# One core, a two-layer convolution and feed-forward kernel: its first filter block loaded in two transfers, and a new hand-written issue order

## The chip, the cores and the metric

The kernel runs on one core of one Trainium2 chip. The metric is device time in microseconds (us) of one execution; three runs of the kernel before took 343.04, 343.35 and 342.95 us, and the median, 343.04 us, is the number that counts. Engine names are those of the profile: PE is TensorE's matmul side and PEld its weight loads, DVE is VectorE, ACT is ScalarE, POOL is GpSimd and SP is SyncE, which here issues nearly all the DMAs.

## The reference

Activations `x` are 2048 rows of 512. Two identical layers are applied, each with a long convolution (A) and a feed-forward net (B):

```
def _A_ref(q, k, v, shift_k, ssm_k, ssm_D):
    k_shift = sum over t of k_pad[:, t:t + S, :] * shift_k[:, ks - 1 - t]      # 4 taps
    kv = k_shift * v
    y = irfft(rfft(pad(kv)) * rfft(pad(ssm_k)))[:S]                            # causal, length S
    return q * (y + kv * ssm_D)
def _B_ref(x, w_gate, w_up, w_down):
    return (silu(x @ w_gate) * (x @ w_up)) @ w_down

x = A_q
x = x + _A_ref(_layernorm(x), A_k, A_v, A_shift_k, A_ssm_k, A_ssm_D)
x = x + _B_ref(_layernorm(x), B_w_gate, B_w_up, B_w_down)
(the same two lines once more)
```

The two convolutions differ only in their multiplier, the normalised `x`: the filtered `y` is the same in both layers.

## The kernel before

The sequence is cut into four blocks of 512 rows, `c` = 0 to 3. A block of 512 rows lies in a tile as 128 partitions times 4 interleaved rows `r` = 0 to 3. For each block the kernel makes spectra of the filter `h` (tiles `hn`, transposed to `hs`, spectrum `H` or `G`) and of `kv` (tiles `kn`, `kTb`, `vt`, spectrum `X`), multiplies them on DVE (`t`, `Z`), goes back with a second table of sines (`inv`), and gets `Yk`. A layer norm, the product with `Yk` and a second layer norm give `z`; its transpose `zT` is what the feed-forward matmuls read. The feed-forward net runs over 16 units (layer, block, half); its gate and up matmuls write PSUM tiles `pf`, which ACT evacuates to `sg` and `ht`, DVE multiplies the two, and the down matmuls accumulate in `pd`. The spectra of the later blocks are worked out beside the feed-forward units of the earlier ones; only block 0 stands ahead of everything.

**Block 0, the part that the change touches.** SP issues the loads in this order: `h` of block 0 (`load_h`, L346 to L354, one transfer of 512 KB: 128 partitions, four pieces of 512 columns, one piece for each of the four groups `dt` of 128 channels), `k` (`load_k`, L364), `v` (`load_v`, L394), the activations (L398), `h` and `v` of block 1, and `w_gate`. ACT issues the small taps `tapR` and the vector `drow`. PE first turns the taps (L1173), then transposes `h` (L489): 16 transposes of 128x128, for rows `r` in the order 0, 2, 3, 1 four at a time, one for each `dt`. A row's four transposes fill one PSUM tile, which DVE or ACT copies to `hs` (rows 0 and 1 on DVE, rows 2 and 3 on ACT). Then come 16 transposes of `k` (L378), four for each `dt`, each four copied to `kTb` (L384 on ACT, L386 on DVE).

Two kinds of matmuls follow. The eight "products of `h`" (function `half`, L323 with `hs` and `fwd`) are two matmuls of 512 columns each; four of them read rows 0 and 2, four rows 1 and 3; their results are evacuated to `ev` and combined by four butterflies on DVE into `G` (L457 and L459). The 64 matmuls of the short convolution (function `shift_mul`, L323 with `dg` and `kTb`, 128 columns each, 16 for each row) are multiplied into `vt` on DVE (L536, one for each row). From `vt` come 16 pairs of matmuls for the spectrum `X` (function `direct`, L470), and from `X` and `G` the chain of block 0 described above, up to `zT` (L940 on ACT, L938 on DVE) and the first gate or up matmul.

**What sets the order.** The kernel is written as a list of 1556 operations, in the order of the `add` calls. Each has an engine, a cost and, for a DMA, a latency (`LH0` 3.6 for the first `h`, `LK0` 4.3 for the first `k`, 6.6 for the first `v`). A table `ORDER` gives every operation its place, and the operations are issued in that order, so each engine's instruction stream is written out by hand; costs and latencies do not reach the chip, with one exception. `issue` puts dummy matmuls on PE (tile `wm`, L1307, operands of ones) where the planned start of an operation lies more than 0.5 us behind the end of the one before it on PE:

```
if start < warm_until and start - t > 0.5:
    ...
                n = int((start - t - (0.35 if 0.0 < t < 8.0 else 0.3)) / 0.106)
                if n > 0:
                    warm(ring, i, n)
```

The code for a first `h` in two transfers is already there, behind the switch `H_SPLIT`:

```
if b == 0 and H_SPLIT:
    for n in range(2):
        sl = slice(2 * n, 2 * n + 2)
        o = add(eng, 0.5, lambda sl=sl: q.dma_start(out=hn[b].t[:, sl], in_=h3[:, sl, 0:L]), w=[(hn[b], (n,))],
                lat=LH0 - 0.75 if n == 0 else LH0 - 0.45, due=due, after=after)
    return o
```

With it, `transpose_h` makes two PE operations of each row, of two transposes each, one for each transfer's two `dt`.

Of the kernel before, what the change touches and what calls it, by code (L numbers as in the profile page):

```python
# [30 lines left out]
LK0 = 4.3  # L31
HQ = 'taps'
X0 = 'direct'
# [5 lines left out]
XVE = "AAAAAAAA"  # L39
# [3 lines left out]
H_SPLIT = False  # L43
# [199 lines left out]
def kernel(  # L243
# [14 lines left out]
    nc = tc.nc  # L258
# [161 lines left out]
    def spectrum(name):  # L420
        return new("s8", name, [P, 4, 2, D], parts=8)
# [919 lines left out]
```

## Time and profile before

| what | value |
|---|---|
| median of three runs | 343.04 us (342.95 to 343.35) |
| the profiled execution, its time | 343.52 us |
| its span, first to last instruction | 341.7 us |
| ACT busy share of the span | 74% |
| DVE busy share of the span | 83% |
| HBM read, written | 12.33 MB, 2.10 MB |

The profile is one execution. Its span lies inside the measured time; 1.82 us of the 343.52 us lie around it. Rows of the timeline give the start in us from the span's start, the length in us, the engine, the line of the kernel, the operation, and what it writes and reads; "x16" means that sixteen like instructions are merged in one row, and a remark in square brackets says how long the engine sat idle ahead of it and what released it. Matmuls are pipelined: the length of a row runs to the end of its last matmul, while the next row can start before that, so the rate of matmuls is best read from the starts of successive rows.

### The profile page before, as it was taken

Reading aid. Unit: us, or ns where it says so; the run is one execution under the profiler, and the core shown is the slowest. Engines: PE = TensorE matmul, PEld = TensorE weight load, DVE = VectorE, ACT = ScalarE, POOL = GpSimd, SP = SyncE. Lnnn points to the kernel's source line nnn. Section 1 sums busy time; section 2 is a strip of 40 time slices with the busy share of each in tenths; the row PEclk is TensorE's granted clock in tenths of the full one; section 3 lists DMA queues with packets and bytes.
Section 4 is the critical chain, followed back from the end, with each engine's and each line's share of the span. In section 5 each row is a group of like instructions: output and inputs, shape, how many; then the busy total and the mean of one; then the engine's idle time right before and its main releaser. Section 6 shows DMA issues by size and latency. Waiting matters only on the chain.

```text
span 341.7 us, 6468 instructions
## 1 busy us (share of the span) xinstructions
PE 337.7 (99%) x2563; PEld 243.7 (71%) x2563; DVE 282.4 (83%) x478; ACT 252.5 (74%) x496; POOL 37.0 (11%) x46
## 2 busy tenths in 40 slices
PE   9999999999999999999999999999999999999996
PEld 7656868768686567868587756868685877777683
DVE  7899999999999999999999999889997533726022
ACT  6899999999978475778999973869675545545451
POOL 4010100102105100103110100101101000001000
PEclk9999999999999999999999999999999999999999
DMA  7999314050215155010100224010101110001001
GB/s 287 326 293 359 59 27 67 0 155 1 34 38 102 31 96 169 2 31 2 33 19 14 48 42 129 0 33 1 33 0 39 39 36 0 16 17 28 20 33 31
DMA packets 42088, 22.95 MB, mean 67 GB/s; under 512 B 33989, under 2 KB 39882, under 8 KB 42058
## 3 DMA queue, kind: packets, MB, share of 16 engines
q1 hardware_dynamic: 41904, 22.49, 26.0%
q8 instruction: 20, 0.33, 0.4%
q14 instruction: 10, 0.08, 0.1%
q10 hardware_dynamic: 154, 0.05, 0.1%
HBM read 12.33 MB, written 2.10 MB: 42 GB/s over the span
## 4 chain that ended last, share of the span: by engine, by line
PE 96%; ACT 3%; issue 0%; ACTq 0%
PE pf L323 57%; PE pd L994 28%; PE ps L323 6%; PE ps L470 2%; ACT H L431 1%; PE wm L1307 1%; PE pt L489 1%; ACT Yk L729 1%; ACT ks L526 0%; ACT n L874 0%; PE pt L378 0%; ACT zT L940 0%; ACT X L431 0%; ACT xc L1052 0%; PE pt L1173 0%
## 5 line engine op out<-in xcount | busy, mean ns | idle before, releaser
L323 PE MATMUL pf<-zT,wg_sb 128*128 128x256 bf16 (+1 forms) x872 | 110.3, 275 | 0.0
L323 PE MATMUL pf<-zT,wu_sb 128*128 128x256 bf16 (+1 forms) x872 | 110.0, 275 | 0.1
L994 PE MATMUL pd<-wd_sb,ht 128*128 128x512 bf16 (+1 forms) x462 | 106.2, 373 | 0.0
L323 PEld LDWEIGHTS <-wu_sb 128*128 128x128 bf16 x872 | 85.3, 98 | 18.9 <-issue 0.6
L323 PEld LDWEIGHTS <-wg_sb 128*128 128x128 bf16 x872 | 85.3, 98 | 17.4
L977 ACT CAST ht<-pf 128x512 bf16<-128x512 f32 x112 | 64.7, 589 | 23.3 <-PE pf L323 22.9
L974 ACT ACTIVATE sg<-pf 128x512 bf16<-128x512 f32 x112 | 66.3, 603 | 20.8 <-PE pf L323 17.3
L994 PEld LDWEIGHTS <-ht 128*128 128x128 bf16 x462 | 45.0, 98 | 44.1
L979 DVE TENSOR_TENSOR ht<-ht,sg 128x1024 bf16<-128x1024 bf16 (+1 forms) x61 | 38.8, 640 | 19.9 <-ACT ht L977 13.8
L826 POOL TENSOR_TENSOR rstd<-ve,nhalf 128x2 f32<-128x2 f32 x24 | 25.0, 1045 | 192.7 <-DVE ve L824 192.7
L821 DVE BATCH_NORM_STATS2 bnst<-xc 128x6 f32<-128x512 bf16 x48 | 31.8, 684 | 0.5
L1075 ACT CAST dn<-pd 128x512 bf16<-128x512 f32 x30 | 17.3, 590 | 17.5 <-PE pd L994 17.5
L431 ACT ACTIVATE X<-ps 128x512 bf16<-128x512 f32 x32 | 19.0, 607 | 10.5 <-PE ps L323 10.0
L1078 DVE TENSOR_TENSOR xc<-xc,dn 128x1024 bf16<-128x1024 bf16 x15 | 10.3, 686 | 16.8 <-ACT dn L1075 16.8
L669 DVE TENSOR_TENSOR t<-X,G 128x2048 bf16<-128x2048 bf16 x18 | 21.9, 1216 | 0.1
L665 DVE TENSOR_TENSOR t<-X,G 128x2048 bf16<-128x2048 bf16 x18 | 21.9, 1217 | 0.0
L855 POOL TENSOR_TENSOR rstd<-ve,nhalf 128x2 f32<-128x2 f32 x8 | 8.4, 1044 | 79.6 <-ACT ve L853 79.6
L679 DVE TENSOR_TENSOR Z<-Z,t 128x2048 bf16<-128x2048 bf16 x12 | 14.7, 1221 | 0.3
L677 DVE TENSOR_TENSOR t<-t,t 128x2048 bf16<-128x2048 bf16 x12 | 14.6, 1219 | 0.2
L431 ACT ACTIVATE H<-ps 128x512 bf16<-128x512 f32 x24 | 14.1, 611 | 0.0
L901 DVE TENSOR_TENSOR n<-n,Yk 128x1024 bf16<-128x1024 bf16 x15 | 10.3, 689 | 3.2 <-ACT n L874 1.9
L323 PE MATMUL ps<-hs,fwd 128*128 128x512 bf16 x40 | 12.7, 379 | 0.1
(103 smaller groups left out, 322.4 us busy)
## 6 DMA issues: line engine op xcount, KB each, us to landing
hn<-in_A_ssm_k_dram SPq DMA_DIRECT2D x4, 512.0 KB, 5.4
vt<-in_A_v_dram SPq DMA_DIRECT2D x4, 512.0 KB, 5.2
xc<-in_A_q_dram SPq DMA_DIRECT2D x4, 512.0 KB, 4.7
out_dram<-xc SPq DMA_DIRECT2D x15, 128.0 KB, 1.8
wg_sb<-in_B_w_gate_dram SPq DMA_DIRECT2D x1, 1792.0 KB
wu_sb<-in_B_w_up_dram SPq DMA_DIRECT2D x1, 1792.0 KB, 8.2
wd_sb<-in_B_w_down_dram SPq DMA_DIRECT2D x1, 1280.0 KB, 11.9
kn<-in_A_k_dram SPq DMA_DIRECT2D x1, 512.0 KB, 4.5
```

The lines of the kernel that those rows point to most:

```text
L323: nc.tensor.matmul(o, lhsT=lhsT, rhs=rhs, start=(n == 0), stop=(n == len(terms) - 1))
L431: add("ACT", act(D), lambda: nc.scalar.activation(out=view(), in_=ps.t[:], func=ACT.Copy, scale=scale), r=[ps], w=[(buf, keys)], conv=conv)
L665: dve(n * D, lambda t1=t1, part=part: nc.vector.tensor_mul(out=t1.t[:], in0=x.t[:, sl, 0, :], in1=g.t[:, sl, part, :]), [(x, key(slots, (0 ...
L669: dve(n * D, lambda t2=t2, part=part: nc.vector.tensor_mul(out=t2.t[:], in0=x.t[:, sl, 1, :], in1=g.t[:, sl, 1 - part, :]), [(x, key(slots ...
L679: dve(n * D, lambda t1=t1, part=part: nc.vector.tensor_add(out=z.t[:, sl, part, :], in0=z.t[:, sl, part, :], in1=t1.t[:]), [t1], [zk], con ...
L821: add("DVE", 0.6, lambda st=st, i=i: nc.vector.bn_stats(out=st.t[:], in_=xs[c].t[:, i, :]), r=[(xs[c], (i,))], w=[st])
L826: add("POOL", pw, lambda: nc.gpsimd.tensor_tensor(out=rstd.t[:], in0=ve.t[:], in1=nhalf.t[:].to_broadcast((P, n)), op=ALU.pow), r=[ve, nha ...
L974: add("ACT", act(D), lambda ps=ps, sl=sl: nc.scalar.activation(out=sg.t[:, sl], in_=ps.t[:], func=ACT.Silu), r=[ps], w=[(sg, (b,))], due=( ...
L977: add("ACT", act(D), lambda ps=ps, sl=sl: nc.scalar.copy(out=ht.t[:, sl], in_=ps.t[:]), r=[ps], w=[(ht, (b,))], due=(us[0], at, 1.5, "a"))
L979: dve(n * m * W, lambda: nc.vector.tensor_mul(out=ht.t[:], in0=ht.t[:], in1=sg.t[:]), [sg], [ht], due=(us[0], (k + n) / NF, 0.0, "h"))
L994: nc.tensor.matmul((pds[o] if not cs.start else pds[HP]).t[:, cs], lhsT=ht.t[:, q, at, o * P:(o + 1) * P], rhs=wt["d"].t[:, ft, cs], start ...
L1075: add("ACT", act(D), lambda o=o: nc.scalar.copy(out=dn.t[:, o, :], in_=pds[o].t[:]), r=[pds[o]], w=[(dn, (o,))], due=(unit, 1.0, 3.0, "h"))
```

## The change

Nothing in the arithmetic changes. These are the edits:

- `H_SPLIT` is switched on. The first `h` is loaded by two DMAs of 256 KB, and each row's transposes become two PE operations. The list grows by five operations, to 1561.
- The planner's latencies of the first `k` and `v` become 4.6 and 5.6.
- The whole table `ORDER` is replaced.
- A setting `X0 == "mix"` is added that is not used: `X0` stays `'direct'`.

```
-LK0 = 4.3
+LK0 = 4.6
...
-H_SPLIT = False
+H_SPLIT = True
...
-    0, 5, 1, 2, 3, 21, 16, 6, 14, 8, 15, 66, 69, 10, 7, 9, 4, 11, 34, 12, 17, 18, 13, 19, 20, 35, 26, 120, 121, 131, 27, 30, 31, 39, 37, 40, 36, 41,
...
+    0, 72, 3, 5, 1, 15, 19, 12, 13, 17, 2, 20, 28, 45, 7, 9, 8, 6, 10, 30, 14, 16, 11, 22, 23, 35, 46, 40, 88, 96, 132, 26, 21, 38, 25, 24, 43, 29,
...
-        return add("SP", 0.6, lambda: nc.sync.dma_start(out=vt[b].t[:], in_=v_t[:, b]), w=[vt[b]], lat=(6.6, 9.0)[b] if b < 2 else 5.5, due=due, after=after)
+        return add("SP", 0.6, lambda: nc.sync.dma_start(out=vt[b].t[:], in_=v_t[:, b]), w=[vt[b]], lat=(5.6, 9.0)[b] if b < 2 else 5.5, due=due, after=after)
...
+        elif X0 == "mix":
+            evx = spectrum("evx")
+            X[0] = spectrum("X0")
+            direct(vt[0], X[0], "pf", eng(XVE[:4]), (0, 2))
...
-        if X0 == "half":
+        if X0 in ("half", "mix"):
```

Read with the numbering of the operations (operation 9 becomes 9 and 10, operations 30, 32, 34 and 36 become two each), the new table gives these streams at the start:

- SP: the second transfer's half of `h` (`dt` 2 and 3) first, then the other half (`dt` 0 and 1), then `k`, `v`, the activations, and the rest in the order of before.
- PE: the taps; `dt` 2 and 3 of row 0 and of row 2 (four transposes); `dt` 0 and 1 of rows 2 and 0; `dt` 0 and 1 of rows 3 and 1; `dt` 2 and 3 of rows 3 and 1; four products of `h` (three of rows 0 and 2, one of rows 1 and 3); 12 transposes of `k`; a fifth product; the last four transposes of `k`; a sixth product; then the short convolution, with the seventh product behind 32 of its 64 matmuls and the eighth behind the last. Before, all 16 transposes of `h` were followed by 12 of `k`, two products, four of `k`, then four products among the first 12 matmuls of the convolution, and two products behind its last.
- DVE: one of the four butterflies of `G` moves ahead of the first `vt` product (L536) and three follow the fourth. Before, none stood ahead of the first, one stood behind it and three behind the fourth.
- PE ahead of the first gate or up matmul: one matmul of block 1's `X` (L323 with `vt`), the eight transposes of `z`, and 16 matmuls of block 1's short convolution. Before, these 16 stood ahead of the transposes of `z`, and two matmuls of `X` behind them.
- POOL clears 64 columns of `kTb` as its second operation of the list, and sets `eps` after the `dg` tiles.

113 rows, old and new, of the table ORDER are left out of this document.

## The prediction

> **What bounds the kernel now.** I read the page's busy shares first, then busy time by stage, then PE's rows of the first 33 us.
>
> ```profile
> span 341.7 us, 6468 instructions
> ...
> PE 337.7 (99%) x2563; PEld 243.7 (71%) x2563; DVE 282.4 (83%) x478; ACT 252.5 (74%) x496; POOL 37.0 (11%) x46
> ```
>
> ```profile
> core 0: us, PE busy (x) PEld busy (x) DVE busy (x) ACT busy (x) POOL busy (x), PEclk, DMA share, GB/s
> 22.00:33.00 11.00, 10.76 (x103) 6.91 (x102) 10.62 (x26) 10.88 (x23) 0.69 (x1) 1.00 1.06 379
> 33.00:100.00 67.00, 67.00 (x512) 49.88 (x511) 66.25 (x109) 64.74 (x133) 7.58 (x9) 1.00 0.28 53
> ```
>
> PE is busy 99% of the span, and all 67.00 us of the second window. From the first gate or up matmul on, PE has no hole to close. The time is therefore that matmul's start, plus the PE work left behind it, plus holes that a new order may open. The windows also warn: from 33 to 100 us DVE (66.25) and ACT (64.74) are nearly as full as PE, so an order has little room there. Between 22 and 33 us ACT and DVE are both all but full, and the first feed-forward unit is waiting for them. What the change can win lies ahead of that, in PE's early rows:
>
> ```profile
> 0.76 2.82 PE L1307 MATMUL wm<-const-bfloat16-1.0 128*128 128x128 bf16 x25 [0.76 <-PEq L1325]
> 3.52 0.28 PE L1173 MATMUL pt<-ident,tapR 4*128 4x4 bf16 x4
> 3.73 0.72 PE L1307 MATMUL wm<-const-bfloat16-1.0 128*128 128x128 bf16 x5
> 4.50 1.86 PE L489 MATMUL pt<-ident,hn 128*128 128x128 bf16 x16
> 6.17 0.96 PE L378 MATMUL pt<-ident,kn 128*128 128x128 bf16 x12
> 6.96 1.03 PE L323 MATMUL ps<-hs,fwd 128*128 128x512 bf16 x4
> ...
> 10.45 3.07 PE L323 MATMUL ps<-dg,kTb 128*128 128x128 bf16 x52
> 13.35 1.03 PE L323 MATMUL ps<-hs,fwd 128*128 128x512 bf16 x4
> 14.21 4.48 PE L470 MATMUL ps<-vt,fwd 128*128 128x512 bf16 x20
> 18.53 0.61 PE L489 MATMUL pt<-ident,hn 128*128 128x128 bf16 x8
> 18.98 1.03 PE L470 MATMUL ps<-vt,fwd 128*128 128x512 bf16 x4
> ```
>
> Three things are to be seen. Up to 4.50 us PE does nothing but dummies and the taps. The 16 transposes of `h` take 1.67 us from start to start (4.50 to 6.17), 0.104 us each, while eight like them take 0.45 us at 18.53, 0.056 each: **up to about 6.17 us PE runs at half its later rate**, although the column of the granted clock says 1.00. So a microsecond won ahead of 6.17 is worth half a microsecond of later work. And behind it the pitches are 0.056 us for a matmul of 128 columns (52 in 2.90 us from 10.45 to 13.35) and 0.215 for one of 512 (four in 0.86 from 13.35 to 14.21).
>
> **The change part by part.**
>
> *The two transfers.* SP's rows and the landing lines of `hn` and of `kn`:
>
> ```profile
> 0.72 0.46 SPq L354 DMA_DIRECT2D hn<-in_A_ssm_k_dram  x1
> 1.24 0.49 SPq L364 DMA_DIRECT2D kn<-in_A_k_dram  x1
> ```
>
> ```profile
> DMA to landing us min/median/max: 3.7/5.4/7.1
> ```
>
> ```profile
> DMA to landing us min/median/max: 4.5/4.5/4.5
> ```
>
> ```profile
> 3.00:3.50 0.50, 0.50 (x6) 0.31 (x3) 0.47 (x4) 0.07 (x1) 0.00 (x0) 1.00 1.06 377
> ```
>
> The whole `h` landed 3.7 us behind its issue, at 4.42, and its first transpose starts at 4.50. Between 3.00 and 3.50 the DMAs moved 377 GB/s, so 256 KB fewer is 0.68 us (262 KB by 377): I put the first half at 3.75. Its ends are 3.75 and 4.42 (no gain from being small). The second half is issued 0.52 later (SP's pitch), behind 256 KB in the same queue. Best it lands with the whole of before less a little, say 4.2; worst at 4.42 + 0.52 = 4.94, if the issue sets it. I take 4.45, since the bytes ahead of it are those of before and the transfers were already running at that rate.
>
> `k` and all loads behind it are issued 0.52 later. `k` landed at 1.24 + 4.5 = 5.74 and would land by 6.3; its first use moves from 6.17 to about 7.6, as four products now stand ahead of it, so the delay is covered by more than 1 us. `v` is first read at 11.10 (row below), 5 us behind that. POOL's 64 columns and `eps` are nothing that anyone waits for near their new places, by the margin of the dummies ahead of PE's first work.
>
> *PE's start.* Only four transposes need the first half; twelve need the second. The five dummies at 3.73 go, because the planner's start of the first transposes is now 0.5 + 3.15 = 3.65, only 0.38 behind its end of the taps (3.27), below the 0.5 that calls dummies in. The taps end near 3.8; four transposes at 0.104 end by 4.3; then PE waits for the second half. From 4.45 twelve transposes take 1.25 us and end at 5.70, against 6.17: 0.47 us at half rate, **0.23 us of full-rate work**. With the ends for the second half it is 0.36 (4.2) or 0 (4.94). The first products then must be ready:
>
> ```profile
> 5.13 0.42 DVE L502 TENSOR_TENSOR hs<-pt,drow 128x512 bf16<-128x512 bf16 x1
> 5.55 1.07 ACT L499 COPY hs<-pt 128x512 bf16<-128x512 bf16 x2 [0.21 <-PE pt L489]
> ```
>
> Rows 0 and 2 are complete after eight transposes, at 4.45 + 0.42 = 4.87. The first row of before began to be copied 0.63 us behind 4.50, that is 0.2 behind its fourth transpose's slot; a copy is 0.42 on DVE or 0.54 on ACT (1.07 for two). So rows 0 and 2 are there by 5.65, when the transposes end. No hole.
>
> *Up to the end of the short convolution.* Before, PE had from 6.17 to 13.35 = 7.18 us for 16 transposes of `k` (0.90), six products (2.58) and 64 convolution matmuls (3.58): 7.06 us, so 0.12 of holes. After, seven products stand there: 7.06 + 0.43 - 0.23 = 7.26, end at 13.43. The end of the convolution does not come earlier, because **the product that was put ahead takes what the transfer gave**. The waits inside (copies of `kTb` behind the later transposes) I put at 0, as two products stand between the transposes and the convolution; without that cover each costs the 0.69 us of a DVE copy at most.
>
> *DVE's chain.* The rows that carry it from there:
>
> ```profile
> 9.45 0.68 DVE L434 TENSOR_SCALAR ev<-ps 128x512 bf16<-128x512 f32 x1
> 11.10 0.69 DVE L536 TENSOR_TENSOR vt<-ps,vt 128x512 bf16<-128x512 f32 x1 [0.96 <-PE ps L323]
> 11.71 0.68 DVE L459 TENSOR_TENSOR G<-ev 128x1024 bf16<-128x1024 bf16 x1
> 12.30 1.94 DVE L536 TENSOR_TENSOR vt<-ps,vt 128x512 bf16<-128x512 f32 x3
> 14.16 0.68 DVE L457 TENSOR_TENSOR G<-ev 128x1024 bf16<-128x1024 bf16 x1
> 15.10 0.69 DVE L457 TENSOR_TENSOR G<-ev 128x1024 bf16<-128x1024 bf16 x1 [0.26 <-ACT ev L431]
> 16.34 1.99 DVE L654 TENSOR_TENSOR t<-X,G 128x1024 bf16<-128x1024 bf16 x3
> ```
>
> The last `vt` product ends at 14.24, set by the convolution's end at 13.35. Then three butterflies, at a pitch of 0.61, and a wait of 0.26 for `ev` lead to 16.34. After, the convolution ends 0.08 later, so `vt` is done at 14.32; the three butterflies stand behind it as before, but their `ev` are ready, since only the eighth product is left and it stands right behind the convolution. 14.32 + 3 x 0.61 = 16.15, 0.19 earlier. `X` is no limit: its matmuls start at 13.43 + 0.43 = 13.86 against 14.21. From 16.34 to the first feed-forward matmul the work of DVE is the same in a slightly other order, so I carry the **0.19 us** through.
>
> *The work left behind.* PE's last rows ahead of the feed-forward net:
>
> ```profile
> 30.27 1.05 PE L323 MATMUL ps<-dg,kTb 128*128 128x128 bf16 x16
> 31.40 0.72 PE L935 MATMUL ptz<-ident,z 128*128 128x128 bf16 x8
> 32.05 0.71 PE L323 MATMUL ps<-vt,fwd 128*128 128x512 bf16 x2
> 32.88 1.91 PE L323 MATMUL pf<-zT,wu_sb 128*128 128x256 bf16 x16
> ```
>
> Here PE has holes: 16 x 0.056 = 0.90 from 30.27 leaves 0.23 ahead of 31.40; eight transposes (0.45) leave 0.20 ahead of 32.05; two matmuls (0.43) leave 0.40 ahead of 32.88. After, the 16 stand behind the transposes of `z` and fill that wait (0.90 of the 1.03 us between 31.85 and 32.88), but one matmul of `X` instead of two is done ahead of the net: **0.22 us of work moves behind its start**.
>
> *The rest of the order* (33 us to the end) is costed at 0, hidden in nothing: PE has no hole to close there and can only lose. *Sum:* -0.19 + 0.22 = +0.03 us. Against the profiled execution that is a span of 341.73 and a time of 343.55; the median of the runs lies 0.48 below that execution, so I predict **343.1**.
>
> [...] By the rows, the half rate ends near 6.17, in a stretch where PE was fed without a hole since 0.76. [...]
>
> **The rivals.**
>
> *Rival 1, slower: the half rate lasts longer.* For it: the dummies at 3.73 go, and PE has holes of perhaps 0.1 and 0.2 us between 3.8 and 4.45. If only unbroken work counts, and as long as before (0.76 to 6.17, 5.41 us), full rate comes at 4.45 + 5.41 = 9.86, 3.69 us later, which costs 1.85 us of PE work, all of it ahead of the convolution's end. Against it: the holes are under a tenth of the stretch. It gives 344.9, and decides as soon as the 128-column pitch is still near 0.104 at 7 us. Chance 0.13.
>
> *Rival 2, slower: the new order stalls PE where all three engines are full.* DVE and ACT have 0.75 and 2.26 us of room in 67. If twice a matmul must wait for the ACT copy that frees its `pf` tile (about 0.6 us), the time is 344.3. Against it: before had none of these. Chance 0.17.
>
> *Rival 3, faster: the holes ahead of the net close.* 0.23 + 0.20 + 0.40 = 0.83 us are open between 30.27 and 32.88, and 0.12 in the convolution. If the reordered DVE and ACT chain delivers `z` earlier by as much as PE has been given, the time falls by up to 0.95, to 342.1. For it: the wait behind the `z` transposes is covered. Against it: DVE and ACT are full there. Chance 0.25.
>
> *Rival 4: the change does not do what it says.* The second half lands at 4.94: transposes end at 6.19, nothing is gained, and the sum is +0.26, 343.3. [...] Chance 0.10.
>
> **How the numbers follow.** My forecast, 343.1 (its own range 342.5 to 343.6), has 0.35; rivals 0.13, 0.17, 0.25 and 0.10. About 0.2% (0.69 us) is what a measurement of this kernel can tell from no change. Same: the forecast and rival 4, 0.45. Faster by more: rival 3, 0.25. Slower by more: rivals 1 and 2, 0.30. The range runs from rival 3's full price, 342.0, to near rival 1, 344.6; about 0.1 is left out on each side.
>
> **What would show it.** Right: first transposes of `h` near 3.8 in a group of four, the rest from about 4.45, done by 5.7; the short convolution over near 13.4; the first `t<-X,G` near 16.15; the first matmul on `zT` near 32.7; no idle PE behind it. Wrong: the second half's transposes at or after 4.9; a 128-column pitch of 0.1 at 7 us (rival 1); PE gaps behind 33 us (rival 2); the first matmul on `zT` ahead of 32.2 (rival 3).

## The result, and the profile after

The changed kernel takes **346.32 us** (median of five executions, 344.92 to 346.80) against 343.04 (342.95 to 343.35) for the kernel before: a ratio of 1.0079, 95% interval 1.0058 to 1.0100. In a second series it took 344.87 (six executions, 344.59 to 346.75) against 343.26, a ratio of 1.0058 (1.0041 to 1.0075). It is slower, and its time now scatters by 2 us. The executions of both series form two groups: six at 344.59 to 345.27, five at 346.02 to 346.80, and none between. The profiled one took 344.92 and belongs to the lower group, so its trace holds only a part of the loss. That part first.

The head of the page and PE's busy row (33 matmul records are missing: there are 2567 weight loads, and before has 2563 of each):

```profile
span 343.0 us, 6450 instructions
...
PE 335.5 (98%) x2534; PEld 242.8 (71%) x2567; DVE 282.2 (82%) x478; ACT 252.4 (74%) x496; POOL 32.2 (9%) x46
```

PE's rows of the first 33 us, in the form of those shown of before:

```profile
3.51 0.29 PE L1174 MATMUL pt<-ident,tapR 4*128 4x4 bf16 x4
4.15 0.51 PE L490 MATMUL pt<-ident,hn 128*128 128x128 bf16 x4 [0.34 <-DMA hn<-in_A_ssm_k_dram]
4.93 0.86 PE L490 MATMUL pt<-ident,hn 128*128 128x128 bf16 x12 [0.28 <-DMA hn<-in_A_ssm_k_dram]
5.86 1.89 PE L324 MATMUL ps<-hs,fwd 128*128 128x512 bf16 x7
7.63 0.84 PE L379 MATMUL pt<-ident,kn 128*128 128x128 bf16 x12
...
13.40 0.59 PE L324 MATMUL ps<-hs,fwd 128*128 128x512 bf16 x2
...
30.91 0.38 PE L324 MATMUL ps<-vt,fwd 128*128 128x512 bf16 x1
31.21 0.72 PE L936 MATMUL ptz<-ident,z 128*128 128x128 bf16 x8
31.77 1.06 PE L324 MATMUL ps<-dg,kTb 128*128 128x128 bf16 x16
32.99 0.49 PE L324 MATMUL pf<-zT,wg_sb 128*128 128x256 bf16 x3 [0.16 <-ACT zT L941]
```

The halves of `h` landed at 4.10 and 4.89. PE idles ahead of each, and yet it is at full rate from the second on: twelve transposes take 0.86 us here, sixteen took 1.86 before. The trace also holds a record of the granted clock that no view prints; the views' column counts the time ahead of its first entry as 1.00. The entry of full rate begins at 4.40 us here, within the first four transposes, and at 6.43 in before, and the pitches change at these points. The short convolution ends at 13.40, as forecast, and the first matmul on `zT` starts at 32.99 instead of 32.88.

Behind 33 us there is one hole. PE's rows near 90 us, and the landing line of `zT` between 85 and 95 us, beside the row of the waits:

```profile
89.30 0.59 PE L324 MATMUL ps<-Z,inv 128*128 128x512 bf16 x2
89.74 1.03 PE L995 MATMUL pd<-wd_sb,ht 128*128 128x512 bf16 x4
91.62 1.05 PE L324 MATMUL pf<-zT,wu_sb 128*128 128x256 bf16 x8 [0.86 <-DMA zT<-z]
```

```profile
PE pf L324 <- DMA zT<-z: 0.9, 1, 0.9
```

```profile
DMA to landing us min/median/max: 2.4/3.3/4.2
```

Four matmuls of 512 columns from 89.74 are done at 90.60, at a pitch of 0.215; the next starts at 91.62. So **1.02 us** are lost to `z`'s second DMA transpose, which was issued at 87.36 and landed 4.2 us later, where 2.4 is usual. The three terms of the profiled execution are then 0.11 (start of the net), 0.22 (the product of `X` that moved behind that start, as forecast) and 1.02: 1.35 of the 1.40 us between 344.92 and 343.52. The 1.6 us that separate the two groups aren't in this trace. The 3.28 us between the medians (346.32 and 343.04) are these 1.40, another 1.40 from the profiled execution up to the median, which lies in the upper group, and 0.48 by which the profiled execution of before lies above its own median.

### The profile page after: what moved, and what is told of

Read it like the earlier page. It is cut to its first block, busy times and chain, and to the rows that moved or that the text cites. A ratio compares the mean times of both kernels' runs of the same rounds, so it can differ in the third digit from the quotient of the medians.

```text
span 343.0 us, 6450 instructions
## 1 busy us (share of the span) xinstructions
PE 335.5 (98%) x2534; PEld 242.8 (71%) x2567; DVE 282.2 (82%) x478; ACT 252.4 (74%) x496; POOL 32.2 (9%) x46
## 4 chain that ended last, share of the span: by engine, by line
PE 89%; DVE 3%; ACT 3%; DMA 2%; issue 1%; SPq 0%; ACTq 0%
PE pf L324 53%; PE pd L995 27%; PE ps L324 6%; PE ps L471 2%; DMA zT<-z 1%; DMA hn<-in_A_ssm_k_dram 1%; DVE Z L675 1%; PE ps L810 1%; DVE m L553 1%; ACT sg L975 1%; ACT H L432 1%; PE pt L490 0%; DVE ht L980 0%; DVE t L666 0%; DVE t L670 0%
## 5 line engine op out<-in xcount | busy, mean ns | idle before, releaser
L995 PE MATMUL pd<-wd_sb,ht 128*128 128x512 bf16 (+2 forms) x440 | 101.2, 372 | 1.3
L827 POOL TENSOR_TENSOR rstd<-ve,nhalf 128x2 f32<-128x2 f32 x24 | 20.3, 849 | 206.5 <-DVE ve L825 188.0
L856 POOL TENSOR_TENSOR rstd<-ve,nhalf 128x2 f32<-128x2 f32 x8 | 8.3, 1038 | 71.8 <-ACT ve L854 71.8
L617 ACT ACTIVATE ka<-kTb,tapF 128x512 bf16<-128x512 bf16 x16 | 12.1, 781 | 0.0
```

The costliest lines, as they stand in the source:

```text
L827: add("POOL", pw, lambda: nc.gpsimd.tensor_tensor(out=rstd.t[:], in0=ve.t[:], in1=nhalf.t[:].to_broadcast((P, n)), op=ALU.pow), r=[ve, nha ...
L995: nc.tensor.matmul((pds[o] if not cs.start else pds[HP]).t[:, cs], lhsT=ht.t[:, q, at, o * P:(o + 1) * P], rhs=wt["d"].t[:, ft, cs], start ...
```

## The experiments

Two theories stood, with a rival to both. **F**: the hole comes from a fetch of PE's instructions. The page counts 20 packets on the instruction queue q8, 0.33 MB, that is 16 KB for each 257, on the mean, of PE's 5134 matmuls and weight loads. That q8 carries PE's instructions is borne out below, where its packets move with the number of PE instructions. One of them began at 88.57 and took 1.6 us, in the middle of the transpose. **C**: the upper group has its full rate later, because PE is idle ahead of the halves (0.5 and 0.4 us in the profiled execution). That idle time can do this was a conjecture. The rival was that the new order behind 30 us is at fault by itself, or the split.

All times in us; the last column counts executions 1.0 us or more above the lowest of the same kernel. The kernel before, run beside them in five series, has 2 such in 77, each measured from the lowest of its series.

| kernel | median | lowest to highest | ratio to before (95%) | 1.0 above lowest |
|---|---|---|---|---|
| after_again | 344.87 | 344.59 to 346.75 | 1.0058 (1.0041 to 1.0075) | 5 of 11, with the first series |
| early_new | 345.21 | 344.64 to 346.39 | 1.0057 (1.0044 to 1.0069) | 2 of 6 |
| late_new | 344.55 | 344.29 to 344.75 | 1.0039 (1.0027 to 1.0051) | 0 of 5 |
| x_vt_late | 344.88 | 343.93 to 346.83 | 1.0058 (1.0036 to 1.0081) | 3 of 6 |
| gate_fill | 345.03 | 344.57 to 345.53 | 1.0053 (1.0038 to 1.0068) | 0 of 6 |
| fetch_late | 344.07 | 343.35 to 346.29 | 1.0042 (1.0024 to 1.0060) | 5 of 12 |
| fill_fetch | 344.51 | 344.24 to 344.55 | 1.0038 (1.0025 to 1.0052) | 0 of 6 |
| before_fetch | 343.10 | 342.62 to 344.98 | 1.0003 (0.9990 to 1.0016) | 2 of 12 |
| before_gap | 344.64 | 343.05 to 345.63 | 1.0035 (1.0021 to 1.0050) | 9 of 12 |
| before_hit | 343.69 | 343.41 to 344.35 | 1.0019 (1.0010 to 1.0027) | 0 of 11 |
| early_fetch | 344.75 | 344.35 to 345.95 | 1.0054 (1.0039 to 1.0068) | 2 of 6 |
| late_fetch | 343.95 | 343.64 to 344.50 | 1.0026 (1.0015 to 1.0038) | 0 of 6 |
| fetch_zt | 345.17 | 344.32 to 346.60 | 1.0071 (1.0047 to 1.0094) | 3 of 6 |
| before_zt | 344.05 | 343.83 to 344.64 | 1.0031 (1.0019 to 1.0043) | 0 of 5 |
| late_fetch_zt | 343.88 | 343.71 to 344.47 | 1.0026 (1.0016 to 1.0035) | 0 of 9 |

### The early part, the late part, and one load

The first four runs. The changed kernel again, without an edit:

> The changed kernel once more, for its scatter and a second profile. Theory T1 (the late order hands z's DMA transposes to PE with less than 1 us of slack, so that each transfer that lands at 4.2 us instead of 2.4 becomes a hole in PE): 345 to 347, and in a profile of a run above 345.5 more than the one hole of 1.0 us behind 33 us, each of them ended by a landing of zT. Rival T2 (the early part, the split and the late k, costs the time): the same time, with the additional time ahead of 33 us.

The early part alone, and the late part alone:

```
 early_new: H_SPLIT = True,  ORDER = first 232 operations of after, then the order of before
 late_new:  H_SPLIT = False, ORDER = first 230 operations of before, then the order of after
```

> The first load in two transfers and the changed kernel's first 232 operations (to about 30 us), then the order of before. T1: 343.0 to 343.6, as the kernel before, and no hole of PE behind 33 us. T2: 345.5 to 346.5.

> The kernel before (one transfer) up to about 30 us, then the order of the changed kernel. T1: 345.0 to 346.5, with PE holes of about 1 us behind 33 us ended by landings of zT. T2: 342.8 to 343.5.

And the load that SP issues right behind the transpose that came late:

```
 SP:  zT<-z 86.07, zT<-z 87.36,
-     vt (block 2) 88.62,
      zT<-z 96.90, zT<-z 98.39
+     vt (block 2)
```

> The changed kernel with one load moved: block 2's vt load, issued at 88.62 right behind two of z's DMA transposes, goes behind the next pair of them (96.9 and 98.4). If that load stretches the landing of the transpose ahead of it (4.22 us instead of 2.42), the landing is 2.4 again and the hole of 1.02 us at 90.4 is gone: 1.0 us faster than the changed kernel. If the instruction fetch at 88.57 stretches it, the hole at 90.4 stays and the time is that of the changed kernel within 0.3.

Neither part is innocent: early_new loses as much as the whole change, late_new two thirds of it. So T1 and T2, which each put it all in one part, both fall. The profiles say why. PE's early rows of early_new and of x_vt_late, both in the upper group (346.39 and 346.21):

```profile
4.70 1.47 PE L490 MATMUL pt<-ident,hn 128*128 128x128 bf16 x12 [0.34 <-DMA hn<-in_A_ssm_k_dram]
5.96 2.34 PE L324 MATMUL ps<-hs,fwd 128*128 128x512 bf16 x5
8.52 0.65 PE L324 MATMUL ps<-hs,fwd 128*128 128x512 bf16 x2 [0.22 <-issue]
```

```profile
5.45 1.47 PE L490 MATMUL pt<-ident,hn 128*128 128x128 bf16 x12 [1.10 <-DMA hn<-in_A_ssm_k_dram]
6.72 2.81 PE L324 MATMUL ps<-hs,fwd 128*128 128x512 bf16 x7
```

The products of 512 columns stand 0.427 apart here, against 0.215 in the profiled execution of after: six of them, one missing from the records, fill 5.96 to 8.52. **Full rate came at about 8.6 us** (8.62 and 8.58 by the clock records), in after at 4.40, in after_again at 6.02, in before at 6.43. At half rate to 8.6, the net starts late: the first matmul on `zT` at 34.49 and 34.71. The upper group is rival 1.

Late_new has no split and no scatter, but it has the hole: 0.55 us at 90.3. It is also there in after_again (0.65) and x_vt_late (0.57), where the load of `vt` no longer stands behind the transpose; that load is not its cause. Early_new, with before's order behind 30 us, has a hole in another place:

```profile
265.41 1.46 PE L995 MATMUL pd<-wd_sb,ht 128*128 128x512 bf16 x6
267.57 1.03 PE L324 MATMUL pf<-zT,wu_sb 128*128 128x256 bf16 x8 [0.71 <-DMA zT<-z]
```

Its transpose was issued at 263.14. Of the 16 parts that signal its end, 15 came between 265.48 and 265.62 and the sixteenth at 267.53. A fetch of PE's instructions, one packet of 16 KB, ran from 265.53 to 266.48; such packets take 0.9 to 1.7 us in the 17 traces. Whether the late part stood behind it is not shown, since the traces don't name a packet's engine.

That is not the only form. In after, all 16 parts of the transpose issued at 87.36 came late, between 91.46 and 91.58. The 17 traces hold 510 transposes of `z`, and the moment at which a PE fetch begins sorts them. Where it began 0.5 to 1.8 us behind the issue (33 cases), all 16 parts came late, the last after 3.0 to 4.2 us. Where it began 1.8 to 2.1 us behind (13 cases), 15 parts were in time and one came after 3.9 to 4.6. Where it began 2.2 to 2.6 us behind (16 cases), 15 transposes landed within 2.6 us and one, that of early_new above, after 4.4. The holes near 90 us are all of the first kind; why all 16 parts are late beside a single packet is not shown. Late landings also go with packets of 8 KB on a second instruction queue, q14: in before, 3.3 us for the transpose issued at 86.07 and 3.2 for that of 166.08, with no fetch on q8 near them.

### Moving the fetches, filling the idle time

If the fetches go by the number of PE instructions (one to 257 on the mean, above), a fetch can be moved without touching order or data, by making the dummies fewer and wider:

```
 first group of dummies, columns of each:
-  after:      (128,) * 25
+  fetch_late: (256,) * 12 + (128,)
+  gate_fill:  (256,) * 4 + (128,) * 17, then (256, 256) behind the taps and (256, 256) behind the first two transposes
+  fill_fetch: (512,) * 4 + (256,) * 4 + (128,), and the same two pairs
-  before:       (128,) * 25
+  before_fetch: (128,) * 10 + (64,) * 30
```

> The changed kernel with PE kept busy around the halves of the first h: two dummies of 256 columns behind the taps and two more behind the first four transposes; four of the first dummies are 256 columns wide instead of pairs of 128, so that the number of PE's instructions stays the same. [...] Rival (the runs above 346 come from the late order, or from landings): the same spread as the changed kernel, some runs at 346 and above. [...]

> The changed kernel with 24 fewer PE instructions at its start and the same PE time: 24 of the first 25 dummies become 12 of 256 columns. Theory F (the hole at 90.4 us comes from a fetch of PE's instructions, 16 KB on one DMA engine, that runs into z's transpose; the fetches come once in 256 PE instructions, so 24 fewer move each of them about 1.6 us later): the fetch at 88.57 moves to about 90.2, the transpose issued at 87.36 lands after 2.4 us instead of 4, the hole is gone, 0.65 to 1.0 us faster than the changed kernel, 343.7 to 344.2 in the runs in which full rate comes early. Rival (the transpose lands late for its own order, the load of vt or the queue): hole and time stay, 344.6 to 345.0 at best.

> Both edits in the changed kernel: PE kept busy around the halves, and 24 fewer PE instructions ahead of the net. Theories C and F: no run above 344.8, median 343.5 to 344.1, no hole behind 33 us; what is left over the kernel before is the 0.22 us of the product that moved behind the start of the net and up to 0.3. If either theory falls, a median above 344.5.

> The kernel before, its order and its load untouched, with 30 more PE instructions at its start and the same columns: 15 of the first dummies become 30 of 64 columns. Theory F: each fetch comes about 2.0 us earlier; that of 89.86 runs into the transpose of z issued at 87.35 (0.99 us of slack) and that of 265.14 into the one issued at 261.45 (0.87 of slack), so one or two holes of 0.5 to 1.1 us appear and the time is 343.6 to 345. Rival (the fetches do no harm): 343.0 to 343.3.

Fetch_late bears out F. DMA queues of after between 88.4 and 90.3 us (packets, MB, share of 16 engines' time), then of fetch_late in the same stretch and between 90.4 and 93:

```profile
q1 hardware_dynamic: 508, 0.12, 99.2%
q8 instruction: 1, 0.02, 5.3%
```

```profile
q1 hardware_dynamic: 567, 0.23, 61.4%
```

```profile
q1 hardware_dynamic: 110, 0.39, 38.1%
q8 instruction: 1, 0.02, 2.2%
```

The fetch has left the stretch, and the packets of the transposes, which took 99% of the engines' time with less data moved, take 61%. The transpose lands in time, and PE goes on without a hole (the landing line of `zT`, and PE's row, both of fetch_late):

```profile
DMA to landing us min/median/max: 2.4/2.4/2.4
```

```profile
90.51 1.04 PE L329 MATMUL pf<-zT,wu_sb 128*128 128x256 bf16 x8
```

It is not one profile alone: of the ten with the changed order behind 30 us, the five that have a fetch beside this transpose land it after 3.7 to 4.2 us, and the other five, this one among them, after about 2.4.

The lower group falls from 344.59–345.27 to 343.35–344.09; the upper one stays (five of twelve, 345.34 to 346.29), as F alone wants it.

Gate_fill does the reverse. Its second pair of dummies came to stand behind the first two transposes, not four as was planned. PE's rows of it:

```profile
3.74 0.61 PE L1318 MATMUL wm<-const-bfloat16-1.0 128*128 128x256 bf16 x2
4.41 0.37 PE L495 MATMUL pt<-ident,hn 128*128 128x128 bf16 x2
4.57 0.63 PE L1318 MATMUL wm<-const-bfloat16-1.0 128*128 128x256 bf16 x2
5.26 1.19 PE L495 MATMUL pt<-ident,hn 128*128 128x128 bf16 x14
6.52 1.89 PE L329 MATMUL ps<-hs,fwd 128*128 128x512 bf16 x8
```

Two idle times of 0.27 us are left where after has 0.5 and 0.4, the products run at full rate, and no execution lies above 345.53, where by C I had set the limit at 345.8; the hole at 91 us stays (1.00). With both edits, fill_fetch has neither an upper group nor a hole: 344.24 to 344.55. I had forecast 343.5 to 344.1 and a limit of 344.5; the median of 344.51 touches the limit. In the profiles its first matmul on `zT` stands at 33.24, against 32.89 in fetch_late; the second half of `h` landed at 5.12 in the one and at 4.38 in the other, so these 0.35 us are not shown to be the price of the dummies.

Before_fetch missed its target. The thirty instructions moved the fetch of 89.86 by 4 us, to 85.82, not by 2, and that of 265.14 to 259.44, and neither cost anything: the transpose issued at 85.68 landed after 3.0 us and was still in time, and the one at 259.82 after 2.4. There is no hole and no loss. It says nothing against F, and nothing for it.

### The same two faults in the kernel before

The sharper test puts each fault into the kernel before, whose order and whose single transfer stay as they are.

```
 before_gap: first dummies (128,) * 20 + (64,) * 10; the five dummies between the taps and h are left out
 before_hit: first dummies (128,) * 20 + (64,) * 10; nothing else
```

> The kernel before without its five dummies between the taps and the first h, so that PE idles there for about 0.7 us; ten of the first dummies are 64 columns wide instead of five of 128, which keeps the count of PE's instructions and so the fetches where they are. Nothing else of the change is in it. [...] Rival (the late runs of the changed kernel belong to the split or the late k): all runs 342.7 to 343.6.

> The kernel before with ten more PE instructions at its start and the same columns: five of the first dummies become ten of 64. Theory F, with the shift per instruction as the last runs showed it (about 0.12 us at 90 us): the fetch of 89.86 comes at about 88.6, into z's transpose issued at 87.35, whose last part lands 1.3 to 1.8 us late against 0.99 us of slack: a hole of 0.3 to 0.8 us near 91 and 343.4 to 344.0, in an order that has no other hole behind 33 us. Rival (fetches do no harm without the changed order): 342.9 to 343.2, no hole.

Before_gap: nine of twelve executions lie at 344.07 to 345.63, three at 343.05 to 343.26. By C I had expected a fifth to a half of them at 344.2 to 345.2; it is more. The profile caught one of the three:

```profile
3.52 0.29 PE L1182 MATMUL pt<-ident,tapR 4*128 4x4 bf16 x4
4.58 1.08 PE L497 MATMUL pt<-ident,hn 128*128 128x128 bf16 x16 [0.77 <-DMA hn<-in_A_ssm_k_dram]
```

Sixteen transposes in 1.08 us instead of 1.86: they run at full rate from the first on. By the clock record full rate came at 3.72, just as the 0.9 us without work (3.67 to 4.58) began, so in this execution it did not come after the idle time. None of the nine late ones has a profile; that their full rate is late is inferred from early_new and x_vt_late. So the idle time does not always cost: here it cost nothing, and full rate was there when it began. Five dummies that compute nothing are worth 1.5 us of the median.

Before_hit gives 343.69 against 343.17, with every execution at or above 343.41. Its hole is not the one near 91 us, where that fetch came at 86.73 and the transpose that it met, issued at 85.99, landed after 3.45 us and still in time, but at 264.7, in the second place that had been worked out for before_fetch. PE's row and the landing line of `zT`; then the queues between 263.3 and 264.9 us in before_hit, and in before:

```profile
265.83 1.05 PE L331 MATMUL pf<-zT,wu_sb 128*128 128x256 bf16 x8 [0.73 <-DMA zT<-z]
```

```profile
DMA to landing us min/median/max: 2.4/3.4/4.4
```

```profile
q1 hardware_dynamic: 134, 0.10, 20.4%
q8 instruction: 1, 0.02, 5.3%
```

```profile
q1 hardware_dynamic: 154, 0.09, 18.5%
```

0.89 us were lost there, in an order that has no hole of its own behind 33 us. Here too 15 of the 16 parts were in time (263.72 to 263.85) and one came at 265.78.

### Each part without the hit

```
 early_fetch = early_new, late_fetch = late_new, each with the first dummies (256,) * 12 + (128,)
```

> The first load in two transfers and the changed kernel's first 232 operations, then the order of before, with 24 fewer PE instructions at the start (24 of the first dummies become 12 of 256 columns), so that no fetch meets a transpose of z. Theories C and F: no hole behind 33 us (there was one of 0.87 at 266.5); 343.2 to 343.8 where full rate comes before 6.5 us, up to 345.4 where it comes at 8.5. If the early part costs time by itself (the k that lands 1 to 2 us later), all runs are above 343.9.

> The kernel before up to about 30 us (one transfer), then the changed order, with 24 fewer PE instructions at the start as above. Theory F: the hole of 0.55 at 90.3 is gone; what is left over the kernel before is the 0.22 us of the product that moved behind the net's start and what the hole ahead of the net adds: 343.3 to 344.0, no run above 344.4, as full rate is never late here. Rival (the late order costs time in another way): 344.3 to 344.8 as before the edit.

Late_fetch loses its hole and 0.5 us: it lies 0.78 above the kernel before of its series, late_new 1.29. Its median, 343.95, is within the forecast; two of its six executions, 344.46 and 344.50, are just above the 344.4 that I had set as the limit. Early_fetch loses the hole at 266.5 but gets another, of 0.78 us at 317.9, where the moved fetch meets the transpose issued at 314.71: moving all 20 fetches at once does not keep them clear of fifteen pairs of transposes. Taken off, that leaves about 344.2 with full rate from 4.24 us on. That is above 343.9, so the early part costs time by itself. Its first matmul on `zT` stands at 33.23; the kernel before with full rate about as early (before_gap, 3.72) has it at 32.44. Of these 0.8 us PE idles 0.5 for `k`:

```profile
5.51 1.89 PE L332 MATMUL ps<-hs,fwd 128*128 128x512 bf16 x8
7.74 0.45 PE L387 MATMUL pt<-ident,kn 128*128 128x128 bf16 x5 [0.34 <-DMA kn<-in_A_k_dram]
```

In nine profiles with the split `k` landed between 6.55 and 8.07, in eight without it between 5.44 and 5.84. With one more transfer ahead of it, it is issued 0.5 us later and lands 0.7 to 2.6 us later. All nine also have the new early order, so the two are not told apart.

### What sets the start of the net

Open was why the first matmul on `zT` came 0.11 later although `t<-X,G` came 0.33 earlier. ACT's rows of after:

```profile
31.72 0.65 ACT L841 ACTIVATE jk<-xc 128x512 bf16<-128x512 bf16 x1
...
32.33 0.61 ACT L941 COPY zT<-ptz 128x512 bf16<-128x512 bf16 x1
```

The new order puts a row sum ahead of the copy for which PE waits. These edits swap them:

```
 ACT, fetch_zt and late_fetch_zt:         ACT, before_zt:
-  jk<-xc, zT<-ptz                       -  ks<-ps, zT<-ptz
+  zT<-ptz, jk<-xc                       +  zT<-ptz, ks<-ps
```

> The changed kernel with 24 fewer PE instructions at its start, and with one operation of ACT moved: the copy zT<-ptz that the first gate and up matmuls wait for (32.33 us) goes ahead of the sum jk<-xc (31.72), which the changed order had put in front of it. Theory A (the first matmul on zT starts no earlier than before, although t<-X,G comes 0.33 us earlier, because ACT's copy of zT stands behind jk): first matmul on zT 0.3 to 0.5 us earlier, at 32.4 to 32.7, and 0.3 faster than the same kernel without the move: 343.1 to 343.8 in the runs with an early full rate. Rival (DVE or the late k sets that start): 32.9 to 33.0 again, 343.4 to 344.1.

> The kernel before with one operation of ACT moved: zT<-ptz (32.20 us) goes ahead of ks<-ps (31.74). Theory A: the copy starts at about 31.87, the first matmul on zT 0.2 to 0.35 us earlier, and 342.7 to 343.0 against 343.05 to 343.2. Rival: no difference, or a loss of up to 0.3 because the ks that was passed delays a product of vt.

> The kernel before up to about 30 us, then the changed order, with 24 fewer PE instructions at the start, and with zT<-ptz on ACT ahead of jk<-xc and of ks<-ps: the hole of 1.21 us ahead of the net shrinks to about 0.6 by theory A, 343.1 to 343.6 against 343.95. Rival: 343.7 to 344.3.

PE's rows of late_fetch_zt:

```profile
32.35 1.03 PE L331 MATMUL pf<-zT,wg_sb 128*128 128x256 bf16 x8 [0.36 <-ACT zT L948]
...
37.40 0.82 PE L331 MATMUL pf<-zT,wu_sb 128*128 128x256 bf16 x6 [0.52 <-ACT sg L982]
```

The start comes at 32.35 instead of 33.05, as theory A says, and yet the time is the same (343.88 against 343.95): 0.68 us are given back at 36.6, where PE waits for ACT's `sg`, behind the sums that were pushed back. In fetch_zt the hole ahead of the net closes as well, 0.62 us appear at 37.3, and `k` came so late in its profile (7.97) that PE idled 1.01 us for it; it gained nothing. Before_zt loses 0.9, where its rival had allowed up to 0.3:

```profile
32.01 0.59 ACT L526 CAST ks<-ps 128x512 bf16<-128x512 f32 x1
```

```profile
32.65 0.38 PE L323 MATMUL ps<-vt,fwd 128*128 128x512 bf16 x1 [0.85 <-ACT ks L526]
```

The `ks` that was passed over is what PE's second `X` matmul needed. ACT's busy time in late_fetch (fourth pair of the columns, behind PE, PEld and DVE) shows the limit:

```profile
22.00:33.00 11.00, 9.87 (x96) 6.52 (x98) 10.62 (x25) 10.95 (x24) 0.69 (x1) 1.00 1.06 374
33.00:40.00 7.00, 6.95 (x64) 6.24 (x64) 6.93 (x10) 6.93 (x18) 1.05 (x1) 1.00 0.11 35
```

From 22 to 40 us ACT is busy 17.88 of 18 us, and DVE little less: what one copy wins the next one loses. No version faster than the kernel before came out of these runs.

## Why the prediction was wrong

*What bounds the kernel* was read rightly: start of the net, plus PE's work, plus holes. Both large losses are terms of that sum.

Two steps failed. *The rest of the order is costed at 0* is the one that failed in the profiled execution; *PE's start* failed as well in the executions of the upper group, to which the median of the first series belongs. To the first: I looked at how full the engines are, and named waits for `pf` tiles (rival 2). The hole came from `zT`'s landing. What I could have read in the trace of before: its zT transposes land 0.3 to 1.0 us ahead of their first use in eight of fifteen cases, and some of them took 3.2 to 4.0 us instead of 2.4, each with an instruction fetch beside it. An order with that little room is only as good as the places in which the fetches fall, and the change moved them, by its order and by the number of dummies. Measured: 0.55 to 1.02 us at 90 us in five profiles, gone when the fetch was moved, and 0.89 in before when a fetch was moved in.

*PE's start* took the end of the half rate near 6.17 as fixed, and so put the loss of the five dummies and the new idle time at nothing. In the two profiles of the upper group full rate came at 8.6 instead, and the first matmul on `zT` at 34.49 and 34.71 instead of 32.88. That is *rival 1, the half rate lasts longer*: it had 0.13 and holds in about half the executions. Its rule was too strict (unbroken work) and its price about right: 1.85 forecast; the means of the two groups lie 1.6 us apart in after and 1.9 in fetch_late. Over all kernels that leave PE idle around `h`, 29 of 59 executions lie 1.0 us or more above their lowest; over the eight that keep it busy, 2 of 60. I had argued against it that the idle time is under a tenth of the stretch.

How much idle time is borne can be read from the starts of PE's matmuls and the clock records. The longest single stretch between the taps and full rate that went with an early full rate is 0.48 us (after, 4.40); the shortest that went with a late one is 0.55 (early_new, 8.62), and x_vt_late had 1.31. In sum, with the short gaps, gate_fill bore 0.59 in pieces and early_new had 0.62 ahead of its products, which run at half rate. Two late profiles are too few to call this a limit. Before itself, which I had read as fed without a hole, stands idle for 0.26 us ahead of 4.50: its five dummies start at 3.73 and, at 0.107 each, are over by 4.24.

Full rate does not come at a fixed moment where PE is kept busy either: the nine profiles of before and of the kernels that do so have it between 3.63 and 6.43, seven of them at 4.21 or later, against 8.6 in the two late ones. The two earliest are late_fetch_zt at 3.63 and before_zt at 3.75: the row of their five dummies at 3.74 is 0.47 us long, that of before 0.72. What sets the moment is in no row.

*The two transfers.* First half: forecast 3.75 (3.75 to 4.42), measured 4.10 in the profile of after and 3.44 to 3.59 in the eight others. Second half: forecast 4.45 (4.2 to 4.94), measured 4.89 there, 4.26 to 5.41 in the others, against 4.05 to 4.54 for the whole. The second half gains nothing on the whole, which is rival 4's condition. `k` was to land by 6.3; it landed at 7.58, the miss of 1.3 us in this step, and that uses up the cover that I had given it.

*Up to the end of the convolution:* 13.43 forecast, 13.40 measured, but by two errors that cancel. The second half landed 0.44 later than I took, but full rate came at 4.40, so the twelve transposes behind it end at 5.63, not 5.70. Then the first product waited 0.23 us for the copies of `hs`, where I had written that there is no hole, and about as much was saved because I had counted time won ahead of 6.17 at half its worth. Before_gap, with full rate at 3.72 and no split, ends its convolution at 12.9.

*DVE's chain:* `t<-X,G` at 16.15 forecast, 16.01 measured. That 0.19 us would be carried through to the net failed: ACT sets that start (32.99, not 32.7). *The product that moved behind the start,* 0.22 us, was right.

*Rival 3* was the mirror of this: late_fetch_zt closes 0.7 us of the holes ahead of the net and gains nothing, so the room that I gave it (0.95 us) was not there. *Rival 4*'s condition was met, its time (343.3) not, for the same two reasons.

*Chances:* slower had 0.30, and the range ended at 344.6. Rivals 1 and 2 were summed as alternatives; the change brought the first in some executions and in both of its profiles a hole behind 33 us in place of the second, from another cause, and both prices add.

## What to carry to other kernels

Keep PE fed with dummies until the first real data is there, and count the price of idle time ahead of the full rate by the chance that it sets full rate back, not by its length alone (here 29 of 59 executions with it lie 1.0 us or more above their lowest, 2 of 60 without). When an order is searched by a model, give each DMA that PE waits for a margin of at least what its slowest landing in the trace needs (here about 2 us, not the 0.3 to 1.0 of the kernel before), since landings were late beside instruction fetches, and these moved with the number of PE instructions (thirty more of them, and the fetch of 89.86 came at 85.82). And profile a kernel whose times fall into two groups more than once: one trace shows one of them.

## What the hardware showed that was not expected

- The trace of the changed kernel holds 20 fetches of PE's instructions, one for each 257 of its 5134 matmuls and weight loads on the mean; each is one packet of 16 KB, and takes 0.9 to 1.7 us in the 17 traces. A DMA transpose of `z` beside which one began 0.5 to 2.1 us after the issue landed after 3.0 to 4.6 us instead of 2.4 (46 of 46 cases in the 17 traces). Where it began less than 1.8 us after the issue, all 16 parts were late (33 cases); where it began 1.8 to 2.1 us after, one of them (13 cases).
- Full rate on PE came at 3.6 to 6.4 us where PE was kept busy and at 8.6 where a stretch of 0.55 us or more of idle time lay ahead of it (two profiles); the changed kernel alone shows 4.40 and 6.02 in its two profiles. The views' column of the granted clock reads 1.00 in all of them, since it starts to count at the trace's first clock entry.
- Where the load of 512 KB was cut in two, the load behind it landed 0.7 to 2.6 us later, though its issue moved by 0.5. Why was not tried.
